# A state-space convolution with its gradient: products of small matrices on quarter tiles of the array, and a program order read from a table

## The chip, the cores and the metric

The kernel runs on one core of one Trainium2 chip. The core has five engines that run side by side and wait for one another by semaphores: TensorE (PE in the profile; its weight loads are PEld), VectorE (DVE), ScalarE (ACT), GpSimd (POOL) and SyncE (SP, which here issues transfers). The metric is the time on the device in microseconds; lower is better.

## The reference

The program computes a layer and all its gradients for one sequence of L = 2048 rows and D = 512 channels, in bf16. The layer normalises the rows, passes them through a state-space convolution and through a dense layer, and multiplies the two:

```python
xn = _layernorm(x, axis=-1)
s = _A_ref(xn, ...)             # convolution along L
g = _silu(_B_ref(xn, w1, w2))   # 512 -> 1792 -> 512
return x + s * g
```

The convolution's kernel K has one entry for each channel d and each lag l, a sum over N = 128 states:

```python
logdA = dt * A
P = jnp.exp(logdA[:, :, None] * l[None, None, :])
K = jnp.einsum("dn,dnl,dn->dl", Cc, P, dB).real
y = irfft(rfft(up) * rfft(Kp))
```

The reference takes the gradient of this with respect to x, the six state-space matrices, log_dt, the skip weights and both dense weights. The program's outputs are the layer's value and these ten gradients.

## The kernel before

**K and its tables.** exp(logdA * l) isn't made for all 2048 lags. The lag is split: E holds the powers for NE = 21 exponents (E_RUNS: 256 to 2048 in steps of 256, 0 to 7, three near 258 and two of 516 and 772), Y those for the 32 multiples of 8 up to 248, made of seven low ones and three high ones (H). Both are complex, for 128 states (the partitions) and one half h of 64 channels of a block b of 128 channels. gen_tables (line 1206) makes the angles (tau times the exponents in ecst), takes their sines on ScalarE, multiplies by magnitudes, and writes E and Y to DRAM (Ed, Yd) for the backward pass. W is E times the weights C*dB (CT). Then K for four channels at a time is one group of matmuls: Y as the weights, 32 lags x 4 channels = 128 columns, and W as the moving operand, 21 exponents x 4 channels = 84 columns. Of the 4 x 4 blocks of channels in the result only the four on the diagonal are wanted; the other three quarters of the product are thrown away.

This is done by a selection: the result is copied out as Xr with the channel a kept apart, and `group` multiplies it by SEL, matrices of zeros and ones that keep the rows of the own channel and shift them:

```python
for kind, e0, e1 in terms:
    for a in range(4):
        nc.tensor.matmul(out=o, lhsT=k.SEL[:, kind, a], rhs=Xr[:, a, e0:e1, :], ...)
```

Twenty-four such matmuls and twelve copies per block put K in order in KE, which goes to DRAM (Kd) in four transfers of 128 KB and comes back as Kb in one.

**The backward scan** (gen_ssm_bwd, line 1628) goes the same way in reverse. The gradient of K (dKd) is read as GE in four transfers, folded by matmuls with shift matrices FO (ssm_fold, line 1488) to 21 sums per channel, Gc, and spread by VectorE to Gb, where each sum stands four times, multiplied by a mask MK that is zero for the rows of the three other channels. ssm_v (line 1535) multiplies Y (turned, YT) with Gb: per channel group q and part c one matmul with 128 rows, 128 weight columns and 168 moving columns (2 x 4 x 21), and one copy to Vb per group. ssm_products (line 1548) multiplies Vb with E to Tp, and ssm_sums adds Tp over the exponents by 21 matmuls with the identity.

**Around it** run the dense layers (ps_h, ps_o forward; ps_da, ps_dx, ps_w backward), the long transforms as matmuls (dft_fwd, dft_inv; ps_s and ps_i, some on half tiles of 64 rows or 64 columns), the gates and the two layer-norm passes. Blocks are woven: the tables of block b beside the convolution of block b - 1 beside the dense layer.

**The order.** Every operation is first recorded (Recorder; so all have one line, 171, in the profile). The class Plan builds the dependences, gives each operation an estimated cost, and simulates the engines with priorities that a backward pass and a list of some 480 seeded nudges set. This settles the order on each engine, which PSUM bank each tile gets (pool pf, eight banks), and for each operation recorded as k.ev or any_affine whether VectorE or ScalarE does it. Half-tile matmuls are kept in pairs; every other operation is planned by itself.

Of the kernel before, what the change touches and what calls it, by code (L numbers as in the profile page):

```python
# [12 lines left out]
ACT = mybir.ActivationFunctionType  # L13
# [14 lines left out]
E_RUNS = [(256, 256, 8), (0, 1, 8), (258, 2, 3), (516, 256, 2)]  # L28
Y_RUNS = [(8, 8, 7), (64, 64, 3)]
E_EXP, Y_EXP = ([first + step * i for first, step, n in runs for i in range(n)] for runs in (E_RUNS, Y_RUNS))  # L30
NE = len(E_EXP)
NP = NE + NE % 2

# [147 lines left out]
class Plan:  # L181


    SETS = {ACT.Exp: "e", ACT.Silu: "s", ACT.Derivative_silu: "d", ACT.Sin: "nsd", ACT.Tanh: "esd"}
    SEM, ROOM, LAND = 80.0, 212832, 1200.0
    SHY = 40.0
    FROM, ROUNDS = (2371995349, 1, 60), 2
    FIRST, LAST = (70000.0, 8000.0, 1500.0, 40.0, 1200.0), (70000.0, 8000.0, 1500.0, 40.0, 1200.0)
    NUDGES = [(1937556689, 1, 4000), (1102290091, 5, 2000), (1835227684, 0, 100), (2751060829, 5, 2000), (3001717801, 3, 100),
# [93 lines left out]
    def __init__(self, nc, tc, free):  # L283
# [126 lines left out]
        for n, d in enumerate(self.pred):  # L410
            for m in d:
                self.succ[m].append(n)
# [1629 lines left out]
```

## Time and profile before

| | us |
|---|---|
| median of 3 runs | 563.62 |
| lowest, highest | 561.6, 566.12 |
| profiled execution, first to last instruction | 563.6 |
| VectorE busy | 524.8 |
| TensorE busy (ends are modelled) | 515.3 |
| ScalarE busy | 432.2 |
| GpSimd busy | 71.6 |

The profile's page gives, for one execution, busy time by engine, the same in slices of the span, the transfers, the chain of work that ended last (followed back from the end, each step to what released it), and the costliest groups of instructions. The trace behind it answers further questions: busy time in given stretches, groups by shape, instructions in order of time. In a group's row the shapes stand as partitions x elements, then the count, the busy time of all in us and the mean of one in ns.

### The profile page before, as it was taken

To read this page: it belongs to the slowest core of one execution; us is meant where nothing else is said; L and a number is where in the kernel's file an instruction comes from. 1 tells how busy PE (TensorE), PEld (TensorE's weight loads), DVE (VectorE), ACT (ScalarE), POOL (GpSimd) and SP (SyncE) were. 2 spreads that over 40 slices of the span, in tenths; PEclk is the share of its full clock that TensorE was granted. 3 is DMA by queue.
4 is the path that set the end of the run, shared out by engine and by line. 5 is a ranking of instruction groups with operands and counts; after the bars stand their busy time and mean duration, and the time that the engine had idled before them with its cause. 6 is when DMAs were issued, how large, how long until landed. Compare 5 with 4: busy or idle time off the path is not lost.

```text
span 563.6 us, 14496 instructions
## 1 busy us (share of the span) xinstructions
PE 515.3 (91%) x5884; PEld 382.6 (68%) x5884; DVE 524.8 (93%) x986; ACT 432.2 (77%) x720; POOL 71.6 (13%) x136
## 2 busy tenths in 40 slices
PE   0699999998989998789999999998998999999997
PEld 0565777777576675575858777677774777777866
DVE  8999999999989899999999998499998899999993
ACT  7989988999999889999969986266085754657542
POOL 6132111100100100000000001000000303113232
PEclk9999999999999999899999999999998999999999
DMA  8978788969979989874699477999889999999793
GB/s 252 378 246 201 262 277 286 279 225 263 288 243 274 344 270 265 246 146 161 197 244 336 165 254 193 242 247 194 248 162 231 202 234 223 289 213 246 212 238 122
DMA packets 169460, 135.17 MB, mean 240 GB/s; under 512 B 115825, under 2 KB 149361, under 8 KB 166833
## 3 DMA queue, kind: packets, MB, share of 16 engines
q1 hardware_dynamic: 162960, 116.15, 79.8%
q0 software_dynamic: 6144, 17.83, 9.5%
q8 instruction: 46, 0.75, 0.6%
q10 hardware_dynamic: 288, 0.26, 0.2%
q14 instruction: 22, 0.17, 0.1%
HBM read 49.68 MB, written 56.76 MB: 189 GB/s over the span
## 4 chain that ended last, share of the span: by engine, by line
PE 34%; DVE 17%; DMA 10%; SPq 4%; ACT 4%; issue 2%; DVEq 0%; ACTq 0%
PE ps_dx L171 7%; PE ps_da L171 7%; PE ps_w L171 6%; DVE Tp L171 6%; PE ps_i L171 5%; SPq L171 4%; PE ps_s L171 3%; DMA dB<-dA 3%; DMA GE<-dKd 2%; PE ps_v L171 2%; DVE Gt L171 1%; DMA Kb<-Kd 1%; DVE g_t L171 1%; DMA YT<-Yd 1%; DVE jk L171 1%
## 5 line engine op out<-in xcount | busy, mean ns | idle before, releaser
L171 PEld LDWEIGHTS <-W 128*128 128x128 bf16 x1008 | 91.3, 99 | 18.7 <-issue 3.7
L171 ACT CAST dA<-ps_s 128x512 bf16<-128x512 f32 x150 | 81.9, 645 | 4.7 <-PE ps_s L171 3.4
L171 PEld LDWEIGHTS <-xn 128*128 128x128 bf16 x512 | 48.1, 99 | 27.3 <-DVE xn L171 18.5
L171 PE MATMUL ps_h<-XT,W 128*128 128x256 bf16 x448 | 61.7, 279 | 0.4 <-DVE XT L171 0.4
L171 PE MATMUL ps_da<-doT,W 128*128 128x256 bf16 x448 | 60.9, 273 | 0.9 <-DVE doT L171 0.9
L171 PE MATMUL ps_w<-YD,a_tok 128*128 128x512 bf16 x224 | 60.6, 384 | 0.0
L171 PE MATMUL ps_o<-W,aT 128*128 128x512 bf16 x224 | 56.8, 379 | 1.7 <-ACT aT L171 1.0
L171 PE MATMUL ps_w<-dh_tok,xn 128*128 128x256 bf16 x448 | 56.1, 273 | 0.0
L171 PE MATMUL ps_dx<-W,dhT 128*128 128x512 bf16 x224 | 55.7, 379 | 0.0
L171 ACT CAST Vb<-ps_v 128x336 bf16<-128x336 f32 x111 | 41.5, 467 | 17.6 <-PE ps_v L171 15.0
L171 DVE TENSOR_TENSOR Tp<-Vb,Eb 128x1344 bf16<-128x1344 bf16 x64 | 52.7, 847 | 0.3 <-ACT Vb L171 0.3
L171 ACT CAST dB<-ps_i 128x512 bf16<-128x512 f32 x83 | 44.3, 627 | 4.8 <-PE ps_i L171 4.4
L171 DVE TENSOR_TENSOR dhT<-ps_da,dhT 128x512 bf16<-128x512 f32 x56 | 37.2, 681 | 5.3 <-PE ps_da L171 5.3
L171 PE MATMUL ps_v<-Gb,YT 128*128 128x168 bf16 x256 | 32.9, 242 | 3.0 <-DMA YT<-Yd 3.0
L171 PEld LDWEIGHTS <-TF 128*128 128x128 bf16 x416 | 28.9, 98 | 7.8 <-DMA Kb<-Kd 3.0
L171 PEld LDWEIGHTS <-aT 128*128 128x128 bf16 x224 | 19.9, 97 | 21.0 <-issue 3.7
L171 PEld LDWEIGHTS <-dhT 128*128 128x128 bf16 x224 | 20.9, 98 | 18.6 <-issue 0.4
L171 PEld LDWEIGHTS <-YD 128*128 128x128 bf16 x576 | 28.0, 98 | 7.2 <-issue 1.9
L171 ACT CAST o<-ps_w 128x512 bf16<-128x512 f32 (+1 forms) x28 | 15.6, 571 | 21.0 <-PE ps_w L171 18.9
L171 PE MATMUL ps_s<-dB,F 128*64 128x512 bf16 x192 | 27.3, 387 | 3.8 <-DMA dB<-dA 3.5
L171 PEld LDWEIGHTS <-a_tok 128*128 128x128 bf16 x224 | 21.0, 99 | 14.3 <-issue 0.2
L171 ACT ACTIVATE dhT<-dhT 128x2048 bf16<-128x2048 bf16 (+1 forms) x16 | 27.9, 1743 | 3.7 <-DVE dhT L171 2.0
(232 smaller groups left out, 1208.6 us busy)
## 6 DMA issues: line engine op xcount, KB each, us to landing
Yd<-YD SPq DMA_DIRECT2D x8, 1024.0 KB, 7.2
Ed<-E SPq DMA_DIRECT2D x8, 672.0 KB, 5.3
Eb<-Ed SPq DMA_DIRECT2D x8, 672.0 KB, 5.6
h_in<-Hd SPq DMA_DIRECT2D x10, 512.0 KB, 5.3
Hd<-hT POOLq DMA_DIRECT2D x8, 512.0 KB, 5.6
dhT<-Hd SPq DMA_DIRECT2D x8, 512.0 KB, 6.3
DHd<-dhT SPq DMA_DIRECT2D x8, 512.0 KB, 7.0
Md<-mag_all SPq DMA_DIRECT2D x8, 496.0 KB, 5.7
```

The lines of the kernel that those rows point to most:

```text
L171: getattr(getattr(nc, engine), op)(*[on(a) for a in args], **{w: on(a) for w, a in kw.items()})
```

## The change

**Quarter tiles.** For K the four channels become four matmuls on four column tiles of the array, each 128 rows x 32 columns, writing 32 partitions each of one PSUM tile: only the wanted blocks are made. The tile ps_k holds 16 channel groups, so Xr is copied once per half block:

```diff
-                        nc.tensor.matmul(out=ps[:, q], lhsT=Y[:, m % 2, q0 + 4 * u + q].rearrange("p j a -> p (j a)"),
-                                         rhs=W[:, m, 4 * u + q].rearrange("p e a -> p (e a)"), start=(m == 0), stop=(m == 3))
+                    for a in range(4):
+                        nc.tensor.matmul(out=ps[32 * a:32 * a + 32, q0 + q], lhsT=Y[:, m % 2, q0 + q, a], rhs=W[:, m, q, :, a],
+                                         start=(m == 0), stop=(m == 3))
```

For V (ssm_v) the four channels become four row tiles, 32 rows x 128 columns each, into four PSUM tiles at once:

```diff
-    for q in range(0, 8, 2):
-        for u in range(2):
-            ps = k.pf.tile([P, 512], F32, name="ps_v", tag="pf")
+    for u in range(0, 8, 4):
+        ps = [k.pf.tile([P, 4, 2, 2, NE], F32, name="ps_v", tag="pf") for _ in range(4)]
+        for q in range(4):
             for c in range(2):
...
+                for a in range(4):
+                    rows = slice(32 * a, 32 * a + 32)
+                    nc.tensor.matmul(out=ps[a][:, q, c], lhsT=YT[rows, c, u + q], rhs=Gw[rows, q0 + u + q], start=True, stop=True)
+        for a in range(4):
+            k.ev(Vb[:, u:u + 4].rearrange("p q c w (e a) -> p (q c w e) a", a=4)[:, :, a], ps[a][:].rearrange("p q c w e -> p (q c w e)"))
```

The partitions now hold a channel's 32 lags together (a j, not j a), in Y, KE, GE and FO.

**No mask products.** SEL, MK and Gb go. K is put in order by 20 matmuls per block with the identity or one of three shift matrices (`taps`), which add up in PSUM what a pair of KE's rows needs, and KE is copied in four pieces of 512. In the backward scan the copies of the folded sums go to Gw, and one product per block adds the weighted half:

```diff
-            nc.vector.tensor_tensor(out=Gb[h][:, w], in0=Gc[:, 16 * h:16 * h + 16].unsqueeze(2).to_broadcast([P, 16, 4, NP]),
-                                    in1=k.MK[:, w].unsqueeze(1).to_broadcast([P, 16, 4, NP]), op=ALU.mult)
+    nc.vector.tensor_tensor(out=Gw[:, :, 1], in0=Gw[:, :, 0], in1=k.rl[:].unsqueeze(1).to_broadcast([P, 32, NE]), op=ALU.mult)
```

**Twenty exponents.** The exponent 0 goes (E_RUNS now `(8, 256, 8), (1, 1, 7), (258, 2, 3), (516, 256, 2)`). K at lag 0 is the sum of C*dB over the states: a matmul of ones with CT makes it, it is kept in row 32 of Dbc, and the skip matmul of the transform, whose matrix row0 now has ones in rows 0 and 32, adds it. In the gradient, ssm_sums adds it from a new small tile G0 by one matmul with row0.

**Tables.** The angles, sines and products of Y's ten exponents and of E's twenty are made in two runs of 640 and 1280 elements (before 1024 and 960). H keeps each high power twice, so that the product with it runs over pairs:

```diff
-        H = tbl.tile([P, 16, 2, 3, 4], BF16, name="H", tag="H")
+        H = tbl.tile([P, 2, 3, 64, 2], BF16, name="H", tag="H")
+        twice = lambda ap: ap.rearrange("p d k -> p k d").unsqueeze(3).to_broadcast([P, 3, 64, 2])
+            TT(out=H[:, c], in0=twice(s_[:, :, 7:]), in1=twice(my[:, :, 7:]), op=ALU.mult)
```

**Transfers.** KE goes to Kd in one transfer and comes back as Kb in four; dK goes to dKd in four and comes back as GE in one (before: four and one, one and four).

**The order.** Plan no longer simulates. Neighbouring matmuls are gathered into steps: four quarter tiles always together, and neighbours of the same form and tile up to an estimated 450 ns:

```diff
+        return max(25.0 if x.tile_size[0] * x.tile_size[1] * 4 > P * P else 44.0, n / 2.4 + 2.5)
```

A table in the text (ORDER) gives the sequence of the 3216 steps, and for each of those that either engine can do a bit that puts it on VectorE (157 have it). PSUM banks are given in that order, the longest free first.

More of the change, by code (lines that the diff above doesn't have):

```diff
@@ L433, in __init__, with gather @@
-        self.other = {n: ("DVE", self.cost_of(self.ins[n], "DVE")) for n in free}
-        self.shy = {}
-        for n, (e, c) in self.other.items():
-            slow = c[0] - self.cost[n][0]
-            self.shy[n, e if slow > 0 else self.eng[n]] = self.SHY * abs(slow)
-        self.lead = [400.0 + (c[0] if e == "Pool" else min(c[0], 330.0)) for c, e in zip(self.cost, self.eng)]
+        self.other = {self.of[n]: "DVE" for n in free}
+    def gather(self):
+        shares, modes = [], []
+        for x in self.ins:
+            size = getattr(x, "tile_size", None) if type(x).__name__ == "InstMatmult" else None
+            rows, columns = size[:2] if size else (P, P)
+            shares.append(rows * columns / (P * P))
+            modes.append({1.0: 0, 0.5: 1, 0.25: 3}[shares[-1]] + (shares[-1] < 1 and columns < P))
+        engines = [x.engine.name for x in self.ins]
+        self.steps, n, length = [], 0, 0.0
+        while n < len(self.ins):
+            step = [n]
+            while modes[n] and len(step) < 1 / shares[n] and step[-1] + 1 < len(self.ins) and modes[step[-1] + 1] == modes[n]:
+                if self.ins[step[-1] + 1].tile_position in [self.ins[m].tile_position for m in step]:
+                    break
+                step.append(step[-1] + 1)
+            more, last = sum(self.stream(self.ins[m]) * shares[m] for m in step if engines[n] == "PE"), self.steps[-1] if self.steps else None
+            spots = lambda u: {i for m in u for i in self.uses[m]}
+            if last and engines[n] == "PE" == engines[last[0]] and modes[n] == modes[last[0]] and spots(last) == spots(step) and length + more <= self.BOUND:
+                last += step
+                length += more
+            else:
+                self.steps.append(step)
+                length = more
+            n = step[-1] + 1
+        N = self.N = len(self.steps)
+        of = self.of = [i for i, step in enumerate(self.steps) for _ in step]
+        same = lambda ns: list(dict.fromkeys(of[n] for n in ns))
+        self.pred = [{of[m] for n in step for m in self.pred[n]} - {i} for i, step in enumerate(self.steps)]
+        self.uses = [list(dict.fromkeys(i for n in step for i in self.uses[n])) for step in self.steps]
+        self.tiles = [(tag, same(u)) for tag, u in self.tiles]
+        self.order = [(same(a), same(b)) for a, b in self.order]
+        self.mode = [modes[step[0]] for step in self.steps]
+        self.eng = [engines[step[0]] for step in self.steps]
@@ L806, in tie @@
         for line in self.best.plan.values():
+            line = [n for i in line for n in self.steps[i]]
             for a, b in zip(line, line[1:]):
@@ L915, in make_consts @@
     k.TF = const.tile([P, 16, 2, 128], BF16, name="TF")
[L916 removed]
+    k.ones = ones = wp.tile([P, 128], BF16, name="ones")
     G.memset(ones[:], 1.0)
@@ L1203, in ssm_weights @@
     nc.vector.tensor_copy(out=k.CT[:, :, 2], in_=k.CT[:, :, 1])
+    first = k.pf.tile([P, 16, 32], F32, name="ps_c", tag="pf")
+    nc.tensor.matmul(out=first[:], lhsT=k.ones[:], rhs=k.CT[:, :, 0], start=True, stop=True)
+    k.ev(k.Dbc[32:33, :].rearrange("o (b a s) -> o b s a", b=4, a=4), first[32:33].rearrange("o (b g) (q a) -> o b (g q) a", b=4, a=4))
 def gen_tables(k, b):
@@ new lines, in gen_tables @@
+        H = tbl.tile([P, 2, 3, 64, 2], BF16, name="H", tag="H")
+        tau = k.tau[:, hs]
+        sy = sines("sy", NY, lambda v: TT(out=v.rearrange("p (d e) -> p d e", e=NY), in0=tau.unsqueeze(2).to_broadcast([P, 64, NY]),
+                                          in1=k.ecst[:, NE:].unsqueeze(1).to_broadcast([P, 64, NY]), op=ALU.mult))
+        yield
+        lows = [Y[:, c].rearrange("p q a j -> p (q a) j") for c in range(2)]
+        my = mag[:, 64 * NE:].rearrange("p (d e) -> p d e", e=NY)
@@ L1265, in gen_tables @@
-            yield
-    def group(o, terms):
-        n = len(terms) * 4
-        i = 0
-        for kind, e0, e1 in terms:
-            for a in range(4):
-                nc.tensor.matmul(out=o, lhsT=k.SEL[:, kind, a], rhs=Xr[:, a, e0:e1, :], start=(i == 0), stop=(i == n - 1))
-                i += 1
-    KE = tbl.tile([P, 8, 8, 32], BF16, name="KE", tag="W", bufs=2)
-    bc = lambda ap, m, n: ap.unsqueeze(2).to_broadcast([P, m, n, 32])
-    ev = k.ev
-    A = k.pf.tile([P, 16, 32], F32, name="ps_e", tag="pf")
@@ new lines, in gen_tables @@
+            yield
+        k.ev(Xr[:, :, 16 * h:16 * h + 16], ps[:].rearrange("p q e -> p e q"))
+        yield
+    KE = tbl.tile([P, 8, 8, 32], BF16, name="KE", tag="KE")
+    for i in range(0, 8, 2):
+        ps = k.pf.tile([P, 2, 8, 32], F32, name="ps_e", tag="pf")
+        terms = taps(i)
+        for n, (kind, e0, e1, rows, t0, t1) in enumerate(terms):
+            if rows is None:
+                out, src = ps[:, :, t0:t1], Xr[:, e0:e1].unsqueeze(2).to_broadcast([P, 2, t1 - t0, 32])
+            elif e1 - e0 > 1:
+                out, src = ps[:, rows, t0:t1], Xr[:, e0:e1]
+            else:
+                out, src = ps[:, rows, t0:t1], Xr[:, e0:e1].to_broadcast([P, t1 - t0, 32])
+            nc.tensor.matmul(out=out, lhsT=k.ident[:] if kind < 0 else k.FO[kind], rhs=src, start=(n == 0), stop=(n == len(terms) - 1))
+        k.ev(KE[:, i:i + 2], ps[:])
@@ new lines, in ssm_fold @@
+    z0 += [(MX, GE[:, 4:8, 4], 4, 8)]
+    z1 = [(ID, GE[:, 1, 6], 1, 2)]
+    for t in (3, 4, 5):
+        z1 += [(ID, GE[:, 1, t], 0, 1), (ID, GE[:, 2:4, t], 2, 4)]
+    Gw = sb.tile([P, 32, 2, NE], BF16, name="Gw", tag="Gw", bufs=2)
+    for e, n, terms in ((0, 16, z0), (16, 4, z1)):
+        ps = k.pf.tile([P, 16, 32], F32, name="ps_g", tag="pf")
+        for i, (st, src, e0, e1) in enumerate(terms):
+            nc.tensor.matmul(out=ps[:, e0:e1], lhsT=k.ident[:] if st < 0 else k.FO[st], rhs=src, start=(i == 0), stop=(i == len(terms) - 1))
+        k.ev(Gw[:, :, 0, e:e + n], ps[:, 0:n].rearrange("p e q -> p q e"))
@@ L1555, in ssm_products, with ssm_sums @@
     return Tp
-def ssm_sums(k, Tp, out):
+def ssm_sums(k, Tp, out, first):
     nc = k.nc
```

671 lines of the change are left out of this document (176 added, 495 removed), and 92 rows, old and new, of the table NUDGES.

## The prediction

> **What bounds the kernel now.** I read the page first (busy shares, then the chain), then busy time by stretches, then groups by form, then the instructions of TensorE in order of time.
>
> ```profile
> span 563.6 us, 14496 instructions
> PE 515.3 (91%) x5884; PEld 382.6 (68%) x5884; DVE 524.8 (93%) x986; ACT 432.2 (77%) x720; POOL 71.6 (13%) x136
> PE 34%; DVE 17%; DMA 10%; SPq 4%; ACT 4%; issue 2%; DVEq 0%; ACTq 0%
> ```
>
> The span equals the median of the runs (563.62 us), so nothing is added around it and every sum below is made against 563.6. Two engines are over 90% busy and the chain changes engine all the time: no single wait ends last. So the question is asked by stage (columns: stretch; its length; then busy time and count of PE, PEld, DVE, ACT, POOL; clock; DMA):
>
> ```profile
> 0.00:25.00 25.00, 6.12 (x37) 4.64 (x38) 23.39 (x70) 21.15 (x35) 11.10 (x37) 1.00 0.97 302
> 55.00:200.00 145.00, 137.77 (x1753) 101.55 (x1752) 138.86 (x200) 132.88 (x214) 13.71 (x18) 1.00 0.91 274
> 200.00:245.00 45.00, 36.66 (x589) 28.23 (x588) 43.88 (x70) 44.10 (x69) 0.56 (x1) 0.96 0.90 244
> 350.00:420.00 70.00, 66.55 (x633) 50.11 (x631) 57.70 (x94) 33.32 (x67) 0.00 (x0) 1.00 1.01 219
> 420.00:520.00 100.00, 96.76 (x908) 69.44 (x906) 95.53 (x224) 62.17 (x120) 20.47 (x37) 0.98 1.07 231
> ```
>
> TensorE's idle time is 18.9 us at the start, 7.2 of 145 while the tables and K are made beside the forward dense layers, 8.3 of 45 in the gates, and 3.5 + 3.2 in the backward scan. In the tables' stage three engines are full together; in the gates VectorE and ScalarE are; in the backward scan TensorE, with VectorE close behind. A change pays only as far as it lightens TensorE, or lightens the engine that makes TensorE wait, in the same stage.
>
> **VectorE's fixed work.** Columns: count | busy us, mean ns.
>
> ```profile
> L171 DVE TENSOR_TENSOR Gb<-Gc,MK 128x1408 bf16<-128x1408 bf16 x16 | 13.6, 883 | 2.9 <-ACT Gc L171 2.7
> L171 DVE TENSOR_TENSOR Tp<-Vb,Eb 128x1344 bf16<-128x1344 bf16 x64 | 52.7, 847 | 0.3 <-ACT Vb L171 0.3
> L171 DVE TENSOR_TENSOR Tp<-Tp 128x1344 bf16<-128x1344 bf16 x32 | 26.7, 846 | 0.0
> L171 DVE TENSOR_TENSOR W<-E,CT 128x2688 bf16<-128x2688 bf16 x16 | 24.8, 1548 | 0.0
> L171 DVE TENSOR_TENSOR E<-sn,mag 128x1024 bf16<-128x1024 bf16 x16 | 10.4, 682 | 0.2 <-ACT sn L171 0.2
> L171 DVE TENSOR_TENSOR E<-sn,mag 128x320 bf16<-128x320 bf16 x16 | 5.0, 316 | 0.0
> L171 DVE TENSOR_TENSOR AR<-tau,ecst 128x1024 int32<-128x1024 f32 x8 | 9.7, 1216 | 0.0
> L171 DVE TENSOR_TENSOR H<-sn,mag 128x192 bf16<-128x192 bf16 x16 | 4.0, 250 | 0.0
> ```
>
> The two E rows give 366 ns for 704 elements, 0.52 ns each. The 16 mask products Gb become one 640-element product per block: 4 x 482 ns = 1.9, so -11.7 us. Twenty exponents for 21 shorten Tp by 64 elements (33 ns x 96 = -3.2) and W by 128 (67 ns x 16 = -1.1). E's two products become one of 1280 (815 ns for 998, x 16 = -2.9). H grows from 192 to 384 elements, and both inputs repeat each element in the innermost dimension: at the E rate 350 ns (+1.6 us), at the rate of the 4-byte AR row (1216/1024 = 1.19 ns each) 456 ns (+3.3); I take +3.3, since no row of this kernel repeats both inputs so. Sum -15.6. The Trainium skill (Vector Engine (DVE) Microarchitecture Reference, section 5.1) says that a two-source op in which one element is read again and again innermost ran at one element a cycle; by that rule too the larger term stands, and without it the sum would be -17.3.
>
> **Work that either VectorE or ScalarE does** (k.ev).
>
> ```profile
> L171 ACT CAST Xr<-ps_k 128x336 bf16<-128x336 f32 x20 | 9.2, 460 | 1.2 <-PE ps_k L171 1.2
> L171 DVE CAST Xr<-ps_k 128x336 bf16<-128x336 f32 x12 | 6.0, 500 | 1.6 <-PE ps_k L171 1.4
> L171 ACT CAST KE<-ps_e x26: 185/362/587, 81.9 to 199.5; 128x128 bf16<-128x128 f32 x5, 128x192 bf16<-128x192 f32 x4, 128x448 bf16<-128x448 f32 x4, 128x384 bf16<-128x384 f32 x4
> L171 DVE CAST KE<-ps_e x22: 178/278/423, 84.6 to 199.2; 128x32 bf16<-128x32 f32 x8, 128x128 bf16<-128x128 f32 x7, 128x192 bf16<-128x192 f32 x4, 128x96 bf16<-128x96 f32 x2
> L171 ACT CAST dA<-ps_s 128x512 bf16<-128x512 f32 x150 | 81.9, 645 | 4.7 <-PE ps_s L171 3.4 <-DMA dB<-dA 1.3
> L171 ACT CAST Vb<-ps_v 128x336 bf16<-128x336 f32 x111 | 41.5, 467 | 17.6 <-PE ps_v L171 15.0 <-issue 1.9 <-DVE Tp L171 0.2
> ```
>
> Xr falls from 32 copies (15.2 us) to 8 of 320 (3.7): -11.5. KE falls from the listed copies (26 x 362 + 22 x 278 ns = 15.5 us by medians) to 16 of 512 (x 645 = 10.3): -5.2. Vb stays at 128 copies, 16 elements shorter: (645 - 467)/176 = 1.0 ns each, -2.0. The new copies (four into G0, one into Dbc) cost about 0.3 each by KE's 128-element ones: +1.5. Sum -17.2. By stage both sums give about -16 us in tables and K, -17 in the backward scan.
>
> **TensorE.** Rows of the order of time: start, length, count. Starts of neighbours give the pace, since lengths hold the tail.
>
> ```profile
> 330.45 1.95 PE L171 MATMUL ps_i<-dB,TI 128*128 128x128 bf16 x32
> 332.24 0.60 PE L171 MATMUL ps_da<-doT,W 128*128 128x256 bf16 x4
> 332.77 1.07 PE L171 MATMUL ps_i<-I,sp_in 64*128 64x128 bf16 x32
> 333.77 1.70 PE L171 MATMUL ps_da<-doT,W 128*128 128x256 bf16 x14
> 335.31 1.03 PE L171 MATMUL ps_dx<-W,dhT 128*128 128x512 bf16 x4
> 104.38 0.78 PE L171 MATMUL ps_k<-W,YD 128*128 128x84 bf16 x16
> 104.99 0.38 PE L171 MATMUL ps_o<-W,aT 128*128 128x512 bf16 x1
> 440.00 0.32 PE L171 MATMUL ps_v<-Gb,YT 128*128 128x168 bf16 x2
> 440.15 0.38 PE L171 MATMUL ps_w<-YD,a_tok 128*128 128x512 bf16 x1
> 366.82 0.34 PE L171 MATMUL G<-GE,ident 128*128 128x32 bf16 x7
> L171 PE MATMUL G<-GE,ident 128*128 128x32 bf16 x20 | 1.4, 177 | 0.0
> 194.51 2.46 PE ps_e L171 x24
> ```
>
> Full tiles go at 1.79/32 = 55.9 ns (N = 128) and 1.54/14 = 110 ns (N = 256), 0.42 ns a column. Thirty-two half tiles (64x128) take 1.00 us: sixteen pairs at 55.9 ns plus 0.10 us of leaving the form, and entering it shows as 0.53 - 4 x 0.110 = 0.09 us. So two tiles run as one, and a change of the array's form costs 0.2 us for the round trip. Narrow full-array matmuls do not go below (0.34 - 0.177)/6 = 27 ns.
>
> K: 512 matmuls at 0.61/16 = 38 ns = 19.5 us become 2048 in 512 groups of four. If four run as one, 27 ns a group (13.8); if only two do, 54 (27.6). I take 44, the constant that the change's own grouping charges, between the two: 22.5, +3.0. V: 256 at 0.15/2 = 75 ns = 19.2 us become 256 groups, 11.3: -7.9 (6.9 to 13.8). The folding by SEL, 4 x 2.46 = 9.8 us, becomes 20 matmuls per block with 2944 columns in all, 1.3 us at the pace above: -4.5. Sum -9.4, bounds -22.5 and -1.8. New changes of form: steps are cut at 450 ns, so K makes 16 (one per W) to 56 (seven steps for each of eight 64-group tiles) excursions and V 16 to 32. I take 24 + 32 = 56 x 0.2 = +11.2 (6.4 to 17.6). TensorE as a whole: +1.8, from -16.1 to +15.8. **So the array is not relieved; what can be gained is its waiting.**
>
> **Start and queues.**
>
> ```profile
> 18.46 1.89 PE L171 MATMUL pt_t<-ident,xn 128*128 128x128 bf16 x16 [18.46 <-DVE xn L171]
> L171 DVE TENSOR_TENSOR SEL<-eq,own x3: 379/380/405, 13.3 to 15.9; 128x512 bf16<-128x512 bf16 x3
> L171 SPq DMA_DIRECT2D Kd<-KE x16: 601/612/970, 85.2 to 201.9; - x16
> L171 SPq DMA_DIRECT2D Kb<-Kd x4: 370/380/632, 90.8 to 206.6; - x4
> ```
>
> TensorE's first matmul waits for VectorE until 18.46; four SEL products stand before it and vanish: -1.4 us. On SP's queue Kd takes 16 issues to 4, Kb 4 to 16, and GE and dKd the same for the gradient: per pair 16 x 0.61 + 4 x 0.38 = 11.3 us becomes about 20 x 0.38 = 7.6. That relief counts only where SP ends last (4% of the chain); I cost it at nothing, hidden by the dense layers' matmuls, and at +1 us per block if Kb's fourth issue is the late one. GpSimd's new selects replace as many old ones in a start where it is busy 11.10 of 25 us: nothing.
>
> **The sum.** Start -1.4. Tables and K: TensorE +3.0 - 4.5 + 4.8 = +3.3 against 7.2 of waiting, while VectorE and ScalarE lose 16 between them: -3. Gates: copies made earlier let ScalarE's gate work start earlier; half of the 8.3 us: -4. Backward scan: TensorE -7.9 + 6.4 = -1.5, VectorE -15, of 6.7 us of waiting over half: -4. Together -12.4: **551 us**. Its own range, with the bounds of groups and excursions, is 543 to 558.
>
> **Rivals.** *The waiting goes altogether* (A): groups at 27 ns and 32 excursions give TensorE -16, and the lighter VectorE ends half of the 7.2 + 8.3 + 6.7 us beside it: 563.6 - 1.4 - 16 - 11 = 535. For it speaks that all three engines are full together; against it, that TensorE waits little as it is. *The lighter engines were not the limit* (B): TensorE +1.8, waits stay since they are for transfers and the chain, only the start pays and half the gates: 560. *Four banks at once* (C, slower): each V unit now fills four of the pool's eight PSUM banks and needs four copies of 467 ns, 1.9 us, before they are free; before, a tile took one bank. The dense layers' matmuls beside it live in the other four. If TensorE waits 0.75 us for each of 32 units, +24 on 551: 575; it outweighs the gain once the mean wait is over (569 - 551)/32 = 0.56 us. Against it: ScalarE is idle 37.8 of 100 us in that stage. The Trainium skill (TensorEngine Tiling (Array Packing), PSUM Bottleneck) warns of this, that after a fourfold packing the copies out of PSUM may become the bound; no run shows it yet. *Four tiles do not run as one* (D): each pays the 27 ns floor, K 55.3 (+35.8), V 27.6 (+8.4), folding -4.5, form changes +11.2: +51, less the gains of 12: 602. Against it, the half tiles. The Trainium skill (TensorE: Matmul & The Clock Gate, Part 1) has a rule for it, starts never closer than about 25 ns however small N is; taken per matmul, K would be 51 us by it, but the pair row, at 31 ns a matmul with N = 128, shows only that a pair is not two matmuls in a row.
>
> **How the numbers follow.** Chances: forecast 0.51, A 0.19, B 0.16, C 0.09, D 0.05. Under 1% (5.6 us) this kernel's measurement can't tell from no change. Faster by over 1%: forecast and A, 0.70; within 1%: B, 0.16; slower: C and D, 0.14. The range takes in A, the forecast and B, with 2 to 6 us for their unknown costs: 533 to 566; C and D are left out.
>
> **What would show it.** Starts of ps_k groups 44 ns apart or less for four (right) or 100 and more (D); ps_e 24 to 20 matmuls and near 1.3 us a block; Gb gone from VectorE and the H product near 456 ns; TensorE's first matmul near 17 us; ps_v units each followed at once by dense matmuls (right) or by waits for Vb (C); gaps of 0.1 us at each change of form, under 60 new ones. The forecast is wrong if TensorE's stream, not its waiting, shortened by by over 10 us, or if its waiting grew.

## The result, and the profile after

The changed kernel takes 611.18 us (median of 4 runs, 610.15 to 613.75) where the kernel before took 563.2 beside it: a ratio of 1.0864, interval 1.0819 to 1.0910. It is 8.6% slower; 551 was forecast, with 566 as the upper end of the range. The profiled execution spans 609.2 us. Ratios here and below are taken over the executions at the usual speed; medians and ranges hold the few slower ones too.

The page of the changed kernel (busy time by engine; the chain that ended last):

```profile
span 609.2 us, 18929 instructions
PE 520.1 (85%) x8131; PEld 378.0 (62%) x8173; DVE 513.6 (84%) x914; ACT 491.1 (81%) x705; POOL 68.6 (11%) x134
PE 12%; ACT 8%; DVE 2%; DMA 2%; issue 1%; SPq 1%; DVEq 0%; ACTq 0%
```

VectorE is lighter by 11.2 us, as meant. TensorE has hardly more work (+4.8), but 89 us in which it does nothing, for 48 before. ScalarE has 59 us more. The chain explains only the last stretch of the program here, so the stages have to tell. Busy time by stretches (columns as in the prediction):

```profile
0.00:25.00 25.00, 11.08 (x86) 9.04 (x87) 20.82 (x59) 20.13 (x18) 8.21 (x33) 1.00 0.87 274
25.00:55.00 30.00, 15.49 (x81) 10.00 (x80) 14.53 (x35) 29.97 (x31) 4.30 (x5) 0.63 0.26 101
55.00:200.00 145.00, 120.04 (x2493) 84.80 (x2504) 121.67 (x152) 116.06 (x165) 15.51 (x24) 0.94 0.75 227
200.00:245.00 45.00, 36.26 (x906) 28.32 (x909) 34.10 (x43) 33.68 (x54) 2.28 (x3) 0.89 0.93 279
420.00:520.00 100.00, 89.39 (x1458) 60.20 (x1468) 89.72 (x203) 93.16 (x134) 10.20 (x19) 1.00 1.08 207
```

and the kernel before in the second of these stretches:

```profile
25.00:55.00 30.00, 28.59 (x253) 20.70 (x252) 28.82 (x67) 27.68 (x38) 8.21 (x11) 1.00 0.79 239
```

Three places stand out. From 25 to 55 us ScalarE is full and TensorE works half the time. From 55 to 245 us no engine is full: TensorE, VectorE and ScalarE all have more idle time than before. From 420 to 520 us ScalarE, which had 37.8 us to spare, has 6.8. (The stretches are cut by time; as the marks below show, the changed kernel is 22 to 44 us behind by then, so a stretch holds somewhat earlier work than before.) The clock granted to TensorE is lower as well, 0.63 and 0.94 in the second and third stretch for 1.00 in both before, and its ps_h matmuls take 296 ns on the mean for 279. The groups of the changed kernel that belong to them (count | busy us, mean ns | idle before, and what ended it):

```profile
L171 ACT ACTIVATE mag_all<-lamr 128x512 bf16<-128x512 f32 x30 | 33.7, 1346 | 0.0
L171 PE MATMUL ps_k<-W,YD 128*32 128x20 bf16 x2048 | 19.8, 180 | 29.6 <-issue 29.6
L171 ACT CAST Vb<-ps_v 128x320 bf16<-128x320 f32 x121 | 93.2, 978 | 8.9 <-PE ps_v L171 4.0 <-issue 3.1 <-ACT Vb L171 0.8
```

The same groups before (that of Vb stands in the prediction):

```profile
L171 ACT ACTIVATE mag_all<-lamr 128x512 bf16<-128x512 f32 x31 | 16.2, 613 | 1.1 <-DVE lamr L171 1.1
L171 PE MATMUL ps_k<-W,YD 128*128 128x84 bf16 x512 | 26.8, 201 | 0.6 <-DVE W L171 0.5
```

The magnitudes took 613 ns each before, the Vb copies 467 (both now write spaced elements), and K's matmuls had no such pauses. Marks in the traces, by the start of the instruction, in us:

| | first K product | last transform of Kb | first ps_da | end |
|---|---|---|---|---|
| before | 56.8 | 222.7 | 245.9 | 563.6 |
| changed | 78.4 | 263.2 | 289.7 | 609.2 |
| difference within the stage | +21.6 | +18.9 | +3.3 | +1.8 |

### The profile page after: what moved, and what is told of

Read it like the earlier page. It is cut to its first block, busy times and chain, and to the rows that moved or that the text cites. A ratio compares the mean times of both kernels' runs of the same rounds, so it can differ in the third digit from the quotient of the medians.

```text
span 609.2 us, 18929 instructions
## 1 busy us (share of the span) xinstructions
PE 520.1 (85%) x8131; PEld 378.0 (62%) x8173; DVE 513.6 (84%) x914; ACT 491.1 (81%) x705; POOL 68.6 (11%) x134
## 5 line engine op out<-in xcount | busy, mean ns | idle before, releaser
L171 PEld LDWEIGHTS <-W 128*128 128x128 bf16 x1008 | 95.0, 101 | 37.2 <-issue 14.4
L171 ACT CAST Vb<-ps_v 128x320 bf16<-128x320 f32 x121 | 93.2, 978 | 8.9 <-PE ps_v L171 4.0
L171 ACT CAST dA<-ps_s 128x512 bf16<-128x512 f32 x150 | 82.3, 637 | 12.6 <-PE ps_s L171 10.6
L171 PE MATMUL ps_h<-XT,W 128*128 128x256 bf16 x448 | 65.3, 296 | 10.0 <-ACT hT L171 8.3
L171 PE MATMUL ps_w<-YD,a_tok 128*128 128x512 bf16 x202 | 53.6, 380 | 4.9 <-ACT a_tok L171 2.5
L171 DVE TENSOR_TENSOR Tp<-Vb,Eb 128x1280 bf16<-128x1280 bf16 x64 | 50.6, 821 | 7.1 <-ACT Vb L171 6.9
L171 PE MATMUL ps_k<-W,YD 128*32 128x20 bf16 x2048 | 19.8, 180 | 29.6 <-issue 29.6
L171 DVE CAST dA<-ps_s 128x512 bf16<-128x512 f32 x42 | 27.9, 686 | 20.3 <-PE ps_s L171 20.0
L171 PEld LDWEIGHTS <-YD 128*32 128x32 bf16 (+1 forms) x2112 | 22.1, 95 | 34.1 <-issue 33.1
L171 ACT ACTIVATE mag_all<-lamr 128x512 bf16<-128x512 f32 x30 | 33.7, 1346 | 0.0
L171 POOL DMA_DIRECT2D Hd<-hT x16 | 14.3, 895 | 152.6 <-ACT hT L171 125.6
```

The costliest lines, as they stand in the source:

```text
L171: getattr(getattr(nc, engine), op)(*[on(a) for a in args], **{w: on(a) for w, a in kw.items()})
```

## The experiments

Every experiment keeps the changed kernel's program order, unless it says otherwise. Where fewer or other matmuls are issued, this is done after the order is set: in the diffs, `skip` leaves a recorded matmul out and `swap` gives it other operands. Differences in us are between medians of runs that were made at different times, each beside the kernel before at 561 to 563 us; where they are worked out from the ratios instead, they come out up to 2 us smaller (13.8 us for the 15.9 of the first run below, 6.6 for the 7.6 of the second, 29 and 30 for the two of K).

**The magnitudes in a row.** The change stores the ten large powers' magnitudes with the exponent innermost, so that each of these activations writes every tenth element, 20 bytes apart. Undone for the write alone; VectorE then reads with the stride:

```diff
-    high = mag[:, :, 64 * NE:].rearrange("p b (d e) -> p e b d", d=64)
+    high = mag[:, :, 64 * NE:].rearrange("p b (e d) -> p e b d", d=64)
...
-        my = mag[:, 64 * NE:].rearrange("p (d e) -> p d e", e=NY)
+        my = mag[:, 64 * NE:].rearrange("p (e d) -> p d e", e=NY)
```

> The changed kernel with one edit: the ten magnitudes of Y are written by ScalarE in the old layout, one exponent's 64 channels together, instead of every tenth element; VectorE reads them with a stride instead (32 small products). Theory S (strided writes are slow): the ten 2.45 us activations and the ten 0.92 us ones behind them go back to 0.61, ScalarE loses about 17 us before 48 us, and since TensorE waits there for ScalarE, the time falls by 12 to 18 us, to 593 to 599. Rival O (the table's order is the cause, since it is fixed and waits for its slowest part anyway): the time falls by less than 5 us.

Measured: 595.28 us (594.0 to 597.85), ratio 1.0618 (1.0574 to 1.0662), 15.9 us under the changed kernel. The groups of this run:

```profile
L171 ACT ACTIVATE mag_all<-lamr 128x512 bf16<-128x512 f32 x30 | 16.0, 617 | 0.0
L171 DVE TENSOR_TENSOR YD<-sy,mag 128x448 bf16<-128x448 bf16 x16 | 15.0, 956 | 4.8 <-ACT sy L171 4.8
```

How the stride delays the start is seen on ScalarE in order of time, in the changed kernel (start, length, count):

```profile
13.06 20.00 ACT L171 ACTIVATE mag_all<-lamr 128x512 bf16<-128x512 f32 x18
32.97 0.57 ACT L171 CAST hT<-ps_h 128x512 bf16<-128x512 f32 x1
41.52 6.27 ACT L171 ACTIVATE mag_all<-lamr 128x512 bf16<-128x512 f32 x5
47.80 1.28 ACT L171 ACT_TABLE_LOAD   x1
49.10 1.91 ACT L171 ACTIVATE aT<-hT 128x2048 bf16<-128x2048 bf16 x1
```

The dense layer's first activation aT waits behind the last magnitude until 49.1 us; before it began at 30.8 us, and in this experiment at 31.3. So this cause is worth 14 to 16 us of time. The repair has a price of its own: VectorE's sixteen products YD go from 442 ns in the changed kernel to 956, +8.2 us.

**Vb in a row.** Each V unit's four copies write every fourth element of Vb, 8 bytes apart. Here each writes a row:

```diff
-            k.ev(Vb[:, u:u + 4].rearrange("p q c w (e a) -> p (q c w e) a", a=4)[:, :, a], ps[a][:].rearrange("p q c w e -> p (q c w e)"))
+            k.ev(Vb[:, u + a].rearrange("p c w x -> p (c w x)"), ps[a][:].rearrange("p q c w e -> p (q c w e)"))
```

> The changed kernel with one edit: each copy from ps_v to Vb writes 320 elements side by side instead of every fourth element; the elements of Vb then stand in another order, so the six state-space gradients and log_dt's are of other products, with all counts and shapes the same. Theory S: the copy falls from 978 ns to about 450, ScalarE loses 55 to 60 us between 410 and 550, where it is 93 us of 100 busy, and the time falls by 15 to 30 us, to 581 to 596. Rival P (four PSUM banks filled at once make the copies wait or slow down, not the stride): the copy stays above 800 ns and the time moves by less than 5 us. Rival O: the copy is fast, the time falls by less than 8 us.

Measured: 603.57 us (599.45 to 604.55), ratio 1.0746 (1.0696 to 1.0796), only 7.6 us less.

```profile
L171 ACT CAST Vb<-ps_v 128x320 bf16<-128x320 f32 x121 | 43.9, 442 | 29.0 <-PE ps_v L171 18.1 <-issue 6.8 <-PE ps_dx L171 2.3
```

The copy's price is shown, 978 ns against 442, 49 us of ScalarE. The size that was expected in time is refuted: the order of the changed kernel hides most of it.

**K with fewer instructions.** Two runs. In the first, only one of K's four products is made, by 512 tile matmuls:

```diff
+                        n = len(nc.ops) - 1
+                        if m:
+                            nc.skip.add(n)
+                        else:
+                            nc.swap[n] = dict(nc.ops[n][3], stop=True)
```

> The changed kernel with three quarters of the K matmuls left out (only the first of the four products m is made, so K and all that hangs on it have other values): 512 instead of 2048, still on column tiles, in the same order. Theory I (TensorE runs out of instructions: 2048 matmuls and 2048 weight loads leave faster than they are fetched): the 29.6 us of idle time before ps_k without a releaser fall below 5 us, and the time falls by 15 to 28 us, to 583 to 596. Rival F (it is the form of the tiles, a drain or a conflict at each of the eight halves): the idle time stays above 20 us, the time falls by less than 8.

In the second, all four, each by one matmul on the full array with 80 columns, as many columns for a group of four channels as the tiles have together:

```diff
+                        n, g = len(nc.ops) - 1, (q0 + q) // 4 * 4
+                        if a:
+                            nc.skip.add(n)
+                        else:
+                            nc.swap[n] = dict(out=ps[:, g:g + 4].rearrange("p q e -> p (q e)"), lhsT=Y[:, m % 2, q0 + q].rearrange("p a j -> p (a j)"),
+                                              rhs=W[:, m, q].rearrange("p e a -> p (e a)"), start=(m == 0), stop=(m == 3))
```

> The changed kernel with each four column-tile matmuls of K replaced by one on the full array (128 weight columns, 80 moving columns; 512 matmuls; the results land over one another, so K has other values). No column tiles of 32 are left, and a quarter of the instructions. Theory I: the idle time before ps_k without a releaser is below 5 us here as without the three products, and the time falls by 8 to 22 us, about 6 us less than there, since 512 full matmuls take about 38 ns each. Rival F: here the idle time goes, there it stays.

Measured: 580.77 us (576.33 to 584.11) and 580.01 us (576.41 to 582.11), ratios 1.0348 (1.0286 to 1.0411) and 1.0328 (1.0269 to 1.0386): 30 and 31 us less, more than was expected (at most 28 and 22). K's group in the first, then in the second:

```profile
L177 PE MATMUL ps_k<-W,YD 128*32 128x20 bf16 x512 | 6.0, 180 | 5.3 <-DVE W L177 5.3
```

```profile
L177 PE MATMUL ps_k<-W,YD 128*128 128x80 bf16 x512 | 20.6, 202 | 1.2 <-DVE W L177 1.0
```

The pauses "<-issue" are gone in both, on tiles and on the full array, with 6.0 us of matmul time and with 20.6. So neither the array's form nor the array's time makes them; the number of instructions does. The second was expected to be 6 us slower than the first and isn't: its 14.6 us more of matmul time cost nothing that shows. With the pauses gone the granted clock between the first K product and the last transform of Kb is 1.00 (second run), where it is 0.93 in the changed kernel. What a pause looks like in the changed kernel, TensorE in order of time:

```profile
96.28 4.09 PE L171 MATMUL ps_h<-XT,W 128*128 128x256 bf16 x36
100.31 1.52 PE L171 MATMUL ps_k<-W,YD 128*32 128x20 bf16 x165
107.18 0.90 PE L171 MATMUL ps_k<-W,YD 128*32 128x20 bf16 x91 [5.35 <-issue]
122.18 1.73 PE L171 MATMUL ps_k<-W,YD 128*32 128x20 bf16 x193
126.36 0.64 PE L171 MATMUL ps_k<-W,YD 128*32 128x20 bf16 x63 [2.45 <-issue]
```

A run of 256 small matmuls starts at full pace, stops in the middle for some us, with no semaphore that the profile shows, and goes on. The page's list of transfer queues has a queue for instructions; its row in the changed kernel, then before:

```profile
q8 instruction: 64, 1.05, 0.7%
```

```profile
q8 instruction: 46, 0.75, 0.6%
```

64 packets of 16,384 bytes; at 64 bytes for an instruction (an estimate from the counts) a packet holds 256, 64 x 256 = 16,384 against 8131 + 8173 = 16,304 instructions of TensorE, and before 46 x 256 = 11,776 against 11,768. So this queue carries TensorE's program. In the trace of the changed kernel its packets never start less than 3.3 us after one another, and the pauses that end at 84.35, 107.18 and 126.36 us end 1.2 to 1.5 us after a packet has landed (82.9, 105.7, 125.1); so do the other five. A packet is 128 matmuls with their weight loads: at one in 3.3 us, 26 ns a matmul. The run above takes (1.52 - 0.18)/165 = 8 ns a matmul, with 0.18 the length of the last one.

The rate is not the whole of it. Counted in TensorE's matmuls and weight loads, the eight pauses lie two, three or four times 255 apart, to within 2: they stand where one packet's instructions end and the next packet's begin (a few other instructions are not in the count). In such a run a packet's instructions last 1.0 to 1.9 us, and the packet that is then missing started only 1.1 to 5.4 us after TensorE had begun the one before it. Before the pause that ends at 107.18 us the previous packet had come 15.7 us earlier, so the 3.3 us were not the limit there: the missing one started at 104.8, when TensorE had already stood for 3 us. What is fetched ahead is too little, and too late, for a run of two packets.

The Trainium skill (Runtime: NRT & Kernel Launch, Instruction fetch mechanics) describes the same blocks, 256 instructions, fetched over a queue of the engine's own while the previous ones run, and holds the cost to be mostly hidden, because dispatch is slower than the refill. The block's size agrees with the counts here; that it is hidden doesn't hold for these runs of matmuls on quarter tiles, 29.6 us of pauses.

**Half of K's products**, m = 0 and 3: 1024 tile matmuls in runs of 128.

```diff
+                        if m in (1, 2):
+                            nc.skip.add(len(nc.ops) - 1)
```

> The changed kernel with two of K's four products left out (1024 tile matmuls of K, in runs of 128; values of K are partial). Theory of instruction supply: TensorE got through 91 to 229 matmuls of a run before it stopped, so it holds some instructions ahead and a run of 128 mostly fits: idle time before ps_k under 5 us, not half of 29.6, and the time within 6 us of e3_kq's, 575 to 588. Rival, a price per tile matmul or per group: about half of the pauses stay, 13 to 17 us, and the time is halfway between, 592 to 600.

Measured: 582.29 us (576.98 to 594.7), ratio 1.0350 (1.0297 to 1.0403), level with the two runs above.

```profile
L177 PE MATMUL ps_k<-W,YD 128*32 128x20 bf16 x1024 | 10.6, 180 | 3.1 <-DVE W L177 2.1 <-issue 0.8
```

0.8 us of pauses, not half of 29.6: it is the length of the run, not a price per matmul. What is held ahead covers a run of 128, one packet, and not one of 256.

**K spread out.** All 2048 matmuls are kept and all values; only the order is other. Behind each of K's steps (30 to 40 matmuls) two steps of the dense layers are put where there are any; what depends on K moves back with it.

```diff
+        sequence = self.spread(sequence, eng)
...
+            put(n)
+            since += dense[n]
+            if late and since >= 2:
+                some()
+                since = 0
```

> The changed kernel, all 2048 tile matmuls of K kept and all values the reference's; only the order is changed: where dense steps follow a run of K's steps, each K step (30 to 40 matmuls) is followed by two dense steps of up to 0.45 us, what depends on K moves behind it. About two thirds of the 68 K steps come to stand alone. Theory of instruction supply (a run of 256 small matmuls with their weight loads outruns a supply that brings one 16 KB packet in some 3.5 us): the idle time in front of ps_k falls from 29.6 to 4 to 15 us; some 40 more changes of form at 0.2 us give 8 back: 590 to 605. Rival, each tile matmul costs what it costs wherever it stands (weights, PSUM columns): the pauses stay near 30 us and the changes of form are added, 612 to 622.

Measured: 616.53 us (614.38 to 618.36), ratio 1.0975 (1.0914 to 1.1035). K's group, and then rows of what TensorE waited for between its first K product and the last transform of Kb (total us, times, longest):

```profile
L171 PE MATMUL ps_k<-W,YD 128*32 128x20 bf16 x2048 | 23.9, 180 | 9.1 <-issue 8.8
```

```profile
PE ps_s L171 <- DMA Kb<-Kd: 9.4, 3, 5.1
PE ps_e L171 <- ACT Xr L171: 1.8, 3, 0.7
PE ps_e L171 <- ACT KE L171: 1.3, 2, 0.7
```

The pauses fell from 29.6 to 8.8 us, as supply by blocks has it, but the time did not: the forecast of 590 to 605 failed. (The time lies where the rival had it, 612 to 622, but the rival's mark, pauses that stay near 30 us, did not come.) TensorE's busy time in that stage rose from 150.2 to 160.2 us (more changes of form, and the granted clock at 0.91 for 0.93), and 9.4 us of waiting for Kb's transfer took the place of pauses, since Kb's chain now starts later. The stage took 190.5 us for 184.8. With the magnitudes in a row as well:

> The order of e7_spread and the magnitudes of e1_mag together; all values the reference's. If the two causes are separate, e7_spread's time less 14 to 18 us: 574 to 591; if the start hides behind K's pauses or the other way round, less than 8 us below e7_spread. The kernel before took 561; nothing here repairs the Vb copies, so above 565 in every theory.

Measured: 602.86 us (600.17 to 605.33), ratio 1.0732 (1.0658 to 1.0805): 13.7 us less than the spread alone, nearly what the magnitudes gave by themselves. The time of 574 to 591 us that was expected failed with the expectation on which it stood.

**All three undone together.**

> The changed kernel with three edits at once: the large powers' magnitudes written in a row by ScalarE (VectorE then reads them with a stride; same values), Vb written in a row (its elements stand in another order, so the gradients of the state-space weights are those of other products), K by 512 full-array matmuls of 80 columns in the place of 2048 tile matmuls (K's values are then not those of the reference). Order and plan of all other steps unchanged. Theory of three separate causes, each in its own stage: the single runs took off 15.9 (magnitudes), 7.6 (Vb) and 31.2 us (K) against 611.2; added up 556.5; by stages 62.3 to the first K matmul, 152.2 to the last Kb transform, about 27 to the first dA matmul and 310.7 from there, 552. So 546 to 560, faster than before or equal, near the 551 that was forecast. Rival, the causes cover each other (with one gone the next engine is late in the same stage): the gains do not add and it stays at 566 to 580.

Measured: 561.58 us (558.16 to 565.29), ratio 1.0003 (0.9958 to 1.0048): level with the kernel before, between the 546 to 560 that was expected and the rival's 566 to 580. The three repairs add up to what they gave one by one within 5 us (54.7 by their sum, 49.6 together), but the forecast's gain isn't there. The stage of K, and the longest wait of TensorE there:

```profile
55.00:200.00 145.00, 131.09 (x1703) 97.92 (x1717) 144.58 (x160) 131.02 (x195) 14.18 (x20) 0.99 0.87 265
```

```profile
PE ps_k L177 <- DVE W L177: 7.9, 6, 2.1
```

VectorE is full, 144.6 of 145 us, with 14 of the sixteen products of the repaired read, and so most of its 8.2 us, among its work. Hence the next run.

**The same without the price on VectorE**: it reads the magnitudes in a row too (the edit against the run before).

```diff
-        my = mag[:, 64 * NE:].rearrange("p (e d) -> p d e", e=NY)
+        my = mag[:, 64 * NE:].rearrange("p (d e) -> p d e", e=NY)
```

> As e5_all, but VectorE reads the large powers' magnitudes in a row too, as if they had not been re-ordered, so the tables hold products of other pairs (values differ from here on). That takes away the 8 us that the repair of e1_mag laid on VectorE (16 products YD at 956 ns for 443). Theory: e5_all ended level with the kernel before because VectorE was full where K is made (144.6 of 145 us, TensorE waiting 7.9 us for W), partly by this price; without it the forecast's gain appears, 552 to 557, with under 4 us of TensorE waiting for W. Rival, the lighter engines were not the limit there (the forecast's rival B): 559 to 563, as e5_all.

Measured: 554.64 us (551.58 to 561.52), ratio 0.9868 (0.9832 to 0.9904), 1.3% faster than before; the profiled execution spans 551.3. The same two rows:

```profile
55.00:200.00 145.00, 135.34 (x1765) 100.44 (x1780) 142.59 (x168) 137.06 (x202) 14.26 (x20) 0.99 0.91 283
```

```profile
PE ps_k L177 <- DVE W L177: 2.1, 4, 0.8
```

8 us less on VectorE gave 6.9 us of time (7.6 by the ratios): in that stage VectorE binds once TensorE's pauses are gone.

**V on the full array**, beside the three repairs: 256 matmuls of 160 columns for 1024 on four row tiles.

```diff
+                    n = len(nc.ops) - 1
+                    if a:
+                        nc.skip.add(n)
+                    else:
+                        nc.swap[n] = dict(out=... ps[q][:, 2 * c:2 * c + 2], lhsT=YT[:, c, u + q],
+                                          rhs=Gw[:, q0 + u:q0 + u + 4], start=True, stop=True)
```

> As e5_all, and V by 256 full-array matmuls of 160 columns in the place of 1024 four-row tile matmuls of 40 (its values are then other sums). Theory that row tiles run as four at once but pay a change of form: 256 groups lose about 160 x 0.42 = 67 ns against some 33, +9 us of TensorE, and some 32 excursions at 0.2 us go, -6: within 5 us of e5_all either way. Rival, V's small matmuls starve TensorE of instructions as K's did: 8 to 25 us faster than e5_all. Rival two, TensorE was relieved by the row tiles as forecast and binds there: 4 to 10 us slower than e5_all.

Measured: 559.9 us (556.97 to 565.34), ratio 0.9960 (0.9921 to 1.0000), not to be told from the 561.58 with row tiles. V's group, here and with the row tiles:

```profile
L177 PE MATMUL ps_v<-Gw,YT 128*128 128x160 bf16 x256 | 22.8, 233 | 0.0
```

```profile
L177 PE MATMUL ps_v<-Gw,YT 32*128 32x40 bf16 x1024 | 12.2, 176 | 2.1 <-DMA YT<-Yd 2.1
```

The tiles shorten the group by 10.6 us of busy time, while TensorE as a whole differs by 3.7 (504.5 with tiles, 508.2 without), and the time not at all.

**The suspects laid on the kernel before.** First, its magnitudes written at every tenth element:

> The kernel before with one edit: ScalarE writes the ten large powers' magnitudes at every tenth element, as the changed kernel does, while VectorE reads the tile as it did (the pairs multiplied are then others, from the tables on). Theory: the ten take 2.5 us for 0.61, those behind each 0.92: +20 us of ScalarE in a stretch where TensorE and VectorE have nothing else, +14 to +20: 576 to 584, and the first aT activation near 48 us for 30.8. Rival, the start is hidden by transfers: below 570.

Measured: 607.56 us (602.84 to 609.69), ratio 1.0821 (1.0773 to 1.0869), far more than expected, and not a clean run: that kernel plans its order itself, from the tiles' overlaps too, and laid it anew. Seven of the magnitudes now stand between other work of ScalarE:

```profile
38.85 2.48 ACT L171 ACTIVATE mag_all<-lamr 128x512 bf16<-128x512 f32 x1
40.83 0.93 ACT L171 CAST hT<-ps_h 128x512 bf16<-128x512 f32 x1
41.65 2.49 ACT L171 ACTIVATE mag_all<-lamr 128x512 bf16<-128x512 f32 x1
```

It confirms the price of one (2.5 us) and says nothing of its worth in time. It also shows that the instruction behind one is lengthened: hT's copy takes 0.93 us there and 0.57 in the changed kernel's rows above.

Second, its Vb copies written at every fourth element; here the order on every engine stays the same:

```diff
-            k.ev(Vb[:, q + u].rearrange("p c w (e a) -> p (c w) e a", a=4), ps[:, 0:336].rearrange("p (x a e) -> p x e a", a=4, e=NE))
+            k.ev(Vb[:, q + u].rearrange("p c w (e a) -> p (c w) a e", a=4), ps[:, 0:336].rearrange("p (x a e) -> p x a e", a=4, e=NE))
```

> The kernel before with one edit: its 128 Vb copies write every fourth element and read PSUM in a row, where they wrote in a row and read every 20th; same values, same count, same places. Theory from e2_vb (52 us of ScalarE were worth only 8 of time): copies near 1.0 us for 0.467, ScalarE +58 us, most of it in idle time (37.8 of 100 us there): 566 to 578. Rival, the copies are on TensorE's path (four banks or one): over 585. Rival two, nothing to be seen: under 564.

Measured: 588.9 us (587.53 to 591.57), ratio 1.0507 (1.0462 to 1.0553). The group of copies, and the row of TensorE's waits for them (total us, times, longest):

```profile
L171 ACT CAST Vb<-ps_v 128x336 bf16<-128x336 f32 x111 | 90.7, 1049 | 10.5 <-PE ps_v L171 8.7 <-issue 1.3 <-ACT a_tok L171 0.2
```

```profile
PE ps_v L171 <- ACT Vb L171: 6.4, 20, 0.5
```

The same price per copy costs 28 us in this order and 8 in the changed one. The 566 to 578 that were expected failed; the time is over the 585 that was the mark of the rival in which the copies lie on TensorE's path. Part of it is that V's matmuls wait for a copy 20 times, and that VectorE's products Tp wait for ScalarE's copies 16.9 us in all (0.3 before the edit, 6.9 in the changed kernel); the rest of the difference between the two orders wasn't traced.

Of the variants of the changed kernel that still compute the whole layer, the fastest is the one with the magnitudes in a row, 595.28 us, slower than the kernel before. The 554.64 us show what the new program is worth without its three costs, with K on the full array and not on quarter tiles; how to be rid of all three and keep the values wasn't found here. The new program order by itself wasn't run on the old program, so its share, for or against, is not shown.

## Why the prediction was wrong

**The start (-1.4).** The SEL products are gone and the dense layer's first matmul came 2.1 us earlier (18.7 for 20.8 us); this step was right, and its sum was wrong by omission. (TensorE's very first matmul came at 10.0 us, not near 17: the new order puts transposes of TF ahead.) The step priced what TensorE's first matmul waits for and nothing of ScalarE: the magnitudes' new order in the tile was in the diff and is not in the working. It costs 14 to 16 us.

**Work that either engine does (-17.2).** The step that failed is "Vb stays at 128 copies, 16 elements shorter ... -2.0". It took the duration from a row of copies that wrote a row; the new ones write every fourth element: with VectorE's share (7 copies of 878 ns, 17 of 499 before) 128 copies took 99 us for 50, +49 instead of -2. Two other terms came as priced: KE 16 copies of 608 and 682 ns for 645, Xr 8 copies, most at 427 ns for the 460 used. The one copy into Dbc, priced at about 0.3 us by rows that write in a row, took 2.4 on VectorE: it writes elements 64 bytes apart, the same slip on a small scale. In time, the slip with Vb is worth about 7 us in this order.

**TensorE (+1.8, K at 22.5).** The array was priced rightly and the front of it not at all. Four tiles do run as one: 40 matmuls take (0.45 - 0.18)/10 = 27 ns a group of four in the spread run's shortest rows:

```profile
87.48 0.45 PE L171 MATMUL ps_k<-W,YD 128*32 128x20 bf16 x40
```

That is the lower bound of the prediction, not the 44 it took (in the changed kernel's long runs it is 4 x 8 = 32); the group's 19.8 us of busy time are near the 22.5. The changes of form were fewer than the 56 taken: K's products stand in 10 stretches and V's in 31. The step that failed is "2048 in 512 groups of four", priced as groups: each of the 2048 is an instruction with a weight load beside it, 3072 more of both together, and a run of 256 drains what is held ahead. The pauses are 29.6 us, and 30 us of time by the runs without them. The prediction named "if its waiting grew" as what would prove it wrong; that is what happened. V's step (-7.9, with form changes taking back +6.4) is borne out by the run on the full array: net nothing that can be measured.

**VectorE's fixed work (-15.6).** Four rows of the changed kernel:

```profile
L171 DVE TENSOR_TENSOR Tp<-Vb,Eb 128x1280 bf16<-128x1280 bf16 x64 | 50.6, 821 | 7.1 <-ACT Vb L171 6.9
L171 DVE TENSOR_TENSOR W<-E,CT 128x2560 bf16<-128x2560 bf16 x16 | 23.6, 1489 | 0.3 <-PE ps_k L171 0.3
L171 DVE TENSOR_TENSOR E<-se,mag 128x1280 bf16<-128x1280 bf16 x16 | 12.7, 822 | 1.1 <-ACT se L171 1.1
L171 DVE TENSOR_TENSOR H<-sy,mag 128x384 bf16<-128x384 bf16 x16 | 8.5, 554 | 1.5 <-ACT sy L171 1.5
```

Tp, W and E are within 1 us of their terms, and the mask products are one product of 487 ns a block, for 482 forecast. H at 554 ns is above both rates that were weighed (350 and 456); the magnitudes' layout is not the reason, since it takes 555 in the run that has them in a row. The engine's total fell by 11.2 us.

**The waiting (-3, -4, -4).** In the run without the three costs, the marks of the table above stand at 61.9, 216.9, 244.5 and 551.3 us: +5.1, -10.9, +4.4 and -10.9 against before, -12.3 in all, where -12.4 was forecast. That is no confirmation. The marks are of one execution each; by the ratio the gain is 7.4 us. And the sum is right only by luck of its parts: tables and scan gave more than twice their terms, the gates lost 4.4 where 4 was to be gained, and the first K product comes later than before even there; why, is open. That VectorE and not TensorE decides in K's stage once the pauses are gone, the reverse of rival B, is shown by the 6.9 us. The relief of SP's queue (11.3 to 7.6 us a pair), which was priced at nothing, did not come: it gave each of sixteen issues the 0.38 us of Kb's four, and Kb in sixteen takes 0.63 each.

**The rivals.** The prediction had two slower cases. D (four tiles do not run as one) is refuted by the 27 ns. C (four banks wait for their copies) named the right pair, V and its copies, for the wrong reason: although each copy took twice what it assumed, V's matmuls waited for them only 3.0 us in all:

```profile
PE ps_v L171 <- ACT Vb L171: 3.0, 6, 0.5
```

(The mean wait at which C outweighs the gain is 12.4/32 = 0.39 us; the 0.56 in the prediction is where it makes the kernel 1% slower.) Neither the layout of a write nor the supply of instructions was among the cases, so 0.14 on slower was too little.

## What to carry to other kernels

Read a diff for the layout of every output, not only for shapes and counts: a copy that gathers or scatters elements is priced by a row that does the same, or by both ends, and the engine that writes it may be another than the one that the layout was chosen for. When one matmul becomes several small ones, count instructions and the length of their longest run, and compare the run with the packets in which instructions come in, where the trace shows their queue; time on the array is only one of two terms. And undo suspected costs one by one and then together: only the last shows whether the rest of the change is worth anything.

## What the runs showed of the hardware

ScalarE's price of a spaced 2-byte output was higher at the wider of the two steps here: in an activation 512 elements take 0.62 us in a row and 2.5 at steps of 20 bytes, in a copy 320 elements 0.44 in a row and 0.98 at steps of 8 bytes; VectorE's copies of the latter kind take 0.88 for 0.49. The instruction behind a magnitude written at 20 bytes took 0.91 to 0.95 us for 0.6. The Trainium skill (SBUF — State Buffer, Door 1: The DMA port swizzle, the note on cachelines) tells of 16-byte lines with full speed for two hits or more in a line, which makes a bf16 step free up to 8 elements. The 20-byte step agrees, one hit a line; the 8-byte step does not: with two hits a line it would be free by that rule, and it doubled the time.

TensorE's program comes in packets of 256 instructions that followed one another in no less than 3.3 us. With 256 quarter-tile matmuls in a run TensorE stood still for up to 6.5 us at a time, each time at the end of a packet, until 1.2 to 1.5 us after the next one had landed. Runs of 128 passed with 0.8 us of pauses in all.
